# First projections dt by dt over half-loaded weights, another load order, and a last output tile in two halves, in a gated mix of local attention and a token MLP

## The chip, the core and the metric

The kernel runs on one core of one Trainium2 chip. The metric is the device time of one execution in microseconds (us). A profiled execution also has a span, from the first to the last instruction, which is about 1.7 us shorter than its time. Engines are written as in the profile: PE is the matmul engine, PEld its weight load, DVE the vector engine, ACT the scalar engine, POOL the general one, and SP the engine that issues the DMAs here (SPq is its queue). "Granted clock" is the share of PE's full clock that the throttle allowed, from the clock records of the trace. These begin when full clock is first granted (at 4.5 us in the kernel before); the half-speed matmuls before that are not in its mean, and a trace without such a record counts as 1.0.

Times of two kernels are compared only within the same rounds on the same chip. A ratio is the mean time of one kernel's fast runs over that of the other's of the same rounds, so it is not quite the ratio of the medians that are also quoted.

## The reference, cut to what matters

```python
# x: 2048 x 512 (bf16); 32 heads of 16; a window of 8 keys, two apart
g = sigmoid((x * gate_w).sum(-1))                # gate, one number per row
a = local_dilated_attention(x @ wqkv) @ wo       # softmax over 8 keys
h = layernorm(x)
u = gelu(h.T @ w1 + b1)                          # mixes tokens: 2048 -> 1792
b = (u @ w2 + b2).T                              # 1792 -> 2048
return g * a + (1 - g) * b
```

In the kernel, PE does in this order: transposes of the first 512 rows of x; the projections Q, K and V; bursts that reduce the products q*k (made by DVE) over each head; the first MLP matmul (14 tiles of 16 matmuls, called ph2); the second MLP matmul (16 output tiles of 14 matmuls, ph3), each tile followed by four attention matmuls with `wo` into the same PSUM bank. DVE does the products q*k, the layernorm, the softmax and the products attention*V. ACT evicts PSUM and does gelu and exp. W1 and W2 come in pieces of two tiles each through three buffers, so a later piece is loaded when the matmuls of an earlier one have ended.

## The kernel before

All operations are declared first; a list scheduler then fixes the order of instructions on each engine and DMA queue, from modelled durations, and waits are planned for that order. The order is thus decided when the kernel is built. Cuts are marked with `# ...`.

```python
# the scheduler: of all ready ops, the one that can start first; ties by longest path
k = (st, -bl[op.idx] + 3.0 * op.prio, op.idx)

# loads, in this order on the SP queue
ld_x("sp", 0, 4)
l_wq = ld_w("sp", 0, 0, 4)          # all of Wq
ld_w("sp", 1, 0, 4)                 # all of Wk
ld_x("sp", 4, 4)
ld_xt(1, deps=[l_wq])               # a transposing load of 512 rows
ld_x("sp", 8, 4); ld_xt(2); ld_x("sp", 12, 4); ld_xt(3)
# ...
# Q of the first 512 rows in matmuls of 256 columns, tile by tile
for tp_ in range(2):
    order0 = [(dt, tp_, dl) for dl in range(4) for dt in range(4)]
# ...
bank = main_bank()                  # projections rotate through three PSUM banks
# ...
# softmax: two exps over half the columns each, priced at 1.95 us, table load not priced
last_exp = A("act", ... func=AF.Exp, 1.95, name="sm_exp" + h, prio=0)
# gelu of each ph2 tile: another activation table than exp
A("act", ... func=AF.Gelu_apprx_tanh, 0.72, name="gel_%d" % ft, prio=0)
# attention weights, spread over partitions by DMA from SBUF to SBUF
ld_er(0, 4 * wh, 4, ["att_0", "att_1"], ...)             # chunk 0: waits for both exps
for c in range(1, 4):
    ld_er(c, 0, NW + 1, ["att_0", "att_1", "rs_0", "rs_1"], "er%d" % c, ...)
# W2 pieces; piece 4 and later reuse a buffer and wait for ph3
if i % 2 == 1 and j2 + 3 <= 7:
    ld_w2(j2 + 3)
```

## Time and profile before

| | before |
|---|---|
| time, median of 3 runs | 171.93 us |
| span of the profiled run (its time is 172.55 us) | 170.8 us |
| PE busy / granted clock | 165.0 us (97%) / 1.0 |
| DVE busy | 139.7 us (82%) |
| PE ends, DVE ends | 167.88 us, 161.47 us |

From the page of the kernel before: its header, the busy line, and the 40 equal slices of the span (busy tenths; PEclk is the granted clock in tenths).

```profile
span 170.8 us, 2127 instructions
PE 165.0 (97%) x876; PEld 78.6 (46%) x892; DVE 139.7 (82%) x118; ACT 66.2 (39%) x94; POOL 0.9 (1%) x8
PE   7999989999999999999999999999999999999993
PEclk9999999999999999999999999999999999999999
```

PE bounds the kernel: it is dense nearly everywhere. Two of the four waits of PE in the kernel before (engine and line, what it waited for, total us, times, longest); left out are 1.1 us at the very start and 0.2 us for which the profile names no cause:

```profile
PE ps L586 <- DMA arena<-in_A_x_dram: 0.5, 1, 0.5
PE ps L609 <- DMA arena<-in_A_wqkv_dram: 0.2, 1, 0.2
```

Little can be gained there. The timeline of ACT (start, length, line, operation, output and input, count):

```profile
75.37 1.28 ACT L727 ACT_TABLE_LOAD   x1
76.67 3.71 ACT L727 ACTIVATE arena<-arena 128x2048 bf16<-128x2048 bf16 x2
80.28 1.13 ACT L729 ACTIVATE arena<-arena 128x512 f32<-128x512 f32 x1
81.53 1.28 ACT L789 ACT_TABLE_LOAD   x1
```

Both exps run in a row behind one table load and end at 80.38 (76.67 + 3.71). The timeline of the SP queue: the length is the time that issuing took, not the transfer.

```profile
80.47 4.98 SPq L439 DMA_DIRECT2D arena<-arena  x8
85.49 5.65 SPq L439 DMA_DIRECT2D arena<-in_B_w_dram  x3
91.18 5.21 SPq L439 DMA_DIRECT2D arena<-arena  x4
96.43 0.58 SPq L439 DMA_DIRECT2D arena<-in_B_w_dram  x1
97.06 17.11 SPq L439 DMA_DIRECT2D arena<-arena  x12
114.22 10.02 SPq L439 DMA_DIRECT2D arena<-in_B_w_dram  x3
```

The first line is chunk 0 of the attention weights, released by the exps. Then come the last W1 piece with two W2 pieces, four small DMAs of softmax reciprocals, the third W2 piece, and chunks 1 to 3 of the attention weights. Only then, at 114.22, does the fourth W2 piece get its turn.

The view of this one DMA issue (`--source L439 --window 114.5:115.5`) has its time from issue to landing:

```profile
DMA to landing us min/median/max: 9.0/9.0/9.0
```

By the trace's completion records, which are finer, it landed at 123.19. It was 0.7 us early.

### The profile page before, as it was taken

The page shows a single profiled execution, that of the slowest core. Times are in us where ns is not written, and L with a number is a line of the kernel's source. Part 1 is how long each engine was busy: PE and PEld are TensorE (multiplying, and loading weights), DVE is VectorE, ACT ScalarE, POOL GpSimd, SP SyncE. Part 2 cuts the span into 40 slices and gives each one's busy share as a digit, 9 for nine tenths or more (in the row PEclk, how much of TensorE's full clock was granted, in tenths as well). Part 3 has the DMA queues.
Part 4 walks back from the last instruction along what each step waited for, and adds up shares of the span by engine and source line. Part 5 has one row for each costly group of instructions (what it writes and reads, how often), then busy time and mean ns, then how long its engine had stood idle before and what let it go on. Part 6 is the DMA issues. An engine that isn't in the chain of part 4 may idle for free.

```text
span 170.8 us, 2127 instructions
## 1 busy us (share of the span) xinstructions
PE 165.0 (97%) x876; PEld 78.6 (46%) x892; DVE 139.7 (82%) x118; ACT 66.2 (39%) x94; POOL 0.9 (1%) x8
## 2 busy tenths in 40 slices
PE   7999989999999999999999999999999999999993
PEld 2865544455444444444444444444444444444440
DVE  0745369999979999296999998899999999999800
ACT  3286656966458111569821122000011111122084
POOL 2000000000000000000000000000000000000000
PEclk9999999999999999999999999999999999999999
DMA  5999989960000053443989999998982818001023
GB/s 165 319 144 256 212 228 331 258 181 0 6 0 2 6 155 90 124 125 102 311 235 291 274 328 220 186 196 196 302 236 78 246 43 233 31 31 35 31 92 123
DMA packets 43101, 27.42 MB, mean 161 GB/s; under 512 B 7892, under 2 KB 42324, under 8 KB 42708
## 3 DMA queue, kind: packets, MB, share of 16 engines
q1 hardware_dynamic: 43092, 27.28, 62.5%
q8 instruction: 7, 0.11, 0.3%
q14 instruction: 2, 0.02, 0.0%
HBM read 18.88 MB, written 2.10 MB: 123 GB/s over the span
## 4 chain that ended last, share of the span: by engine, by line
PE 83%; DMA 7%; SPq 6%; ACT 2%; issue 1%
PE ps L776 28%; PE ps L840 28%; PE ps L586 14%; PE ps L849 8%; SPq L460 5%; PE ps L668 4%; DMA arena<-in_A_x_dram 4%; DMA arena<-in_A_wqkv_dram 3%; SPq L439 1%; ACT L564 1%; PE ps L638 1%; ACT arena L867 0%; ACT arena L594 0%; ACT arena L597 0%; ACT arena L564 0%
## 5 line engine op out<-in xcount | busy, mean ns | idle before, releaser
L816 DVE TENSOR_TENSOR arena<-arena 128x2048 bf16<-128x2048 bf16 (+2 forms) x32 | 71.5, 2287 | 1.8 <-DMA arena<-arena 1.5
L840 PE MATMUL ps<-arena 128*128 128x512 bf16 x220 | 49.8, 379 | 0.2
L776 PE MATMUL ps<-arena 128*128 128x512 bf16 x218 | 48.5, 379 | 0.3
L586 PE MATMUL ps<-arena 128*128 128x512 bf16 x171 | 38.3, 379 | 1.0 <-DMA arena<-in_A_x_dram 0.5
L661 DVE TENSOR_TENSOR arena<-arena 128x8192 bf16<-128x8192 bf16 x8 | 35.0, 4416 | 1.3 <-ACT arena L597 1.3
L840 PEld LDWEIGHTS ps<-arena 128*128 128x128 bf16 x224 | 21.9, 98 | 26.4
L776 PEld LDWEIGHTS ps<-arena 128*128 128x128 bf16 x224 | 21.7, 98 | 26.8 <-issue 0.8
L867 ACT ACTIVATE arena<-ps,arena 128x512 bf16<-128x512 f32 x16 | 12.4, 778 | 49.8 <-PE ps L849 49.3
L586 PEld LDWEIGHTS ps<-arena 128*128 128x128 bf16 x176 | 19.6, 114 | 19.1 <-ACT arena L594 0.9
L597 ACT ACTIVATE arena<-ps 128x512 bf16<-128x512 f32 x32 | 19.0, 598 | 7.1 <-PE ps L586 6.9
L789 ACT ACTIVATE arena<-ps,arena 128x512 bf16<-128x512 f32 x14 | 9.6, 687 | 30.8 <-PE ps L776 30.7
L551 DVE BATCH_NORM_STATS2 arena<-arena 128x6 f32<-128x512 bf16 x16 | 9.9, 681 | 6.9 <-DMA arena<-in_A_x_dram 6.9
L849 PE MATMUL ps<-arena 128*128 128x512 bf16 x63 | 15.4, 379 | 0.1
L849 PEld LDWEIGHTS ps<-arena 128*128 128x128 bf16 x64 | 6.3, 98 | 7.5
L713 DVE TENSOR_TENSOR arena<-arena 128x256 bf16<-128x256 bf16 (+4 forms) x16 | 7.9, 506 | 2.0 <-ACT arena L727 1.7
L594 ACT ACTIVATE arena<-ps 128x512 bf16<-128x512 f32 x12 | 7.2, 596 | 3.5 <-PE ps L586 3.5
L668 PE MATMUL ps<-arena 128*32 128x512 bf16 x128 | 7.5, 380 | 0.0
L698 ACT ACTIVATE arena<-ps 128x1024 bf16<-128x1024 f32 x4 | 4.0, 1021 | 5.0 <-PE ps L638 3.8
L570 DVE TENSOR_SCALAR arena<-arena 128x512 bf16<-128x512 bf16 x16 | 5.3, 407 | 0.0
L668 PEld LDWEIGHTS ps<-arena 128*32 128x32 bf16 x128 | 3.1, 96 | 4.1 <-DVE arena L713 0.4
L513 PE MATMUL ps<-arena 128*128 128x512 bf16 x9 | 4.0, 603 | 1.1 <-POOL arena L426 1.1
L609 PE MATMUL ps<-arena 128*128 128x256 bf16 x32 | 3.7, 273 | 0.2 <-DMA arena<-in_A_wqkv_dram 0.2
(50 smaller groups left out, 36.4 us busy)
## 6 DMA issues: line engine op xcount, KB each, us to landing
arena<-in_B_w_dram SPq DMA_DIRECT2D x7, 1024.0 KB, 6.4
arena<-in_B_w_dram SPq DMA_DIRECT2D x8, 896.0 KB, 6.8
arena<-arena SPq DMA_DIRECT2D x12, 288.0 KB, 5.9
arena<-in_A_x_dram SPq DMA_DIRECT2D x4, 512.0 KB, 4.9
out_dram<-arena SPq DMA_DIRECT2D x16, 128.0 KB, 1.7
arena<-in_A_wqkv_dram SPq DMA_DIRECT2D x3, 512.0 KB, 4.6
arena<-arena SPq DMA_DIRECT2D x8, 128.0 KB, 3.0
arena<-in_A_wo_dram SPq DMA_DIRECT2D x1, 512.0 KB, 9.2
```

Source lines behind the costliest of these rows:

```text
L460: return q_dma("sp", lambda e: e.dma_start_transpose(dst, src), 2 * SC * D * 2, "d_xt%d" % sb, ["xt_%d_%d" % (dt, sb) for dt in range(4)], ...
L551: A("dve", (lambda t_: (lambda e: e.bn_stats(out=ST6[:, t_, :], in_=X[:, t_, :])))(t), 0.7, reads=["x%d" % t], writes=["st6_%d" % t], name ...
L586: ins = e.matmul(ps[:, bank, :], lhsT=lhsT, rhs=XT[:, sb, dt, :], start=(dt == 0), stop=(dt == 3))
L597: return lambda e: e.activation(out=dst, in_=ps[:, bank, :], func=AF.Copy)
L661: return lambda e: e.tensor_tensor(out=PBL[buf], in0=in0, in1=in1, op=ALU.mult)
L668: ins = e.matmul(ps[32 * c:32 * c + 32, 4 + wl, :], lhsT=RP, rhs=PBL[buf][:, wl, c * 512:(c + 1) * 512], start=(dl == 0), stop=(dl == 3), ...
L776: ins = e.matmul(ps[:, bank, :], lhsT=W1W[:, slot, st, 128 * e_:128 * e_ + 128], rhs=X[:, st, :], start=(st == 0), stop=(st == NST - 1))
L789: A("act", (lambda ft_, bank_: (lambda e: e.activation(out=UT[:, ft_, :], in_=ps[:, bank_, :], func=AF.Gelu_apprx_tanh, bias=col(B1C, ft_) ...
L816: A("dve", lambda e: e.tensor_tensor(out=o_, in0=a_, in1=b_, op=op_), dur, reads=rd, writes=wr, name=nm)
L840: ins = e.matmul(ps[:, bank, :], lhsT=W2S[slot][:, ft, 128 * e_:128 * e_ + 128], rhs=UT[:, ft, :], start=(ft == 0), stop=False)
L849: ins = e.matmul(ps[:, bank, :], lhsT=OT[:, t, 128 * i:128 * i + 128], rhs=WO[:, t, :], start=False, stop=(t == 3))
L867: A("act", (lambda e, i=i, bank=bank: e.activation(out=OUTS[:, i, :], in_=ps[:, bank, :], func=AF.Identity, scale=col(OMG, i), bias=col(C2 ...
```

## The change

The intent: start the first projections when half of the Q weights have landed, keep PE fed until the transposed rows arrive, keep the evictions from stopping PE, and shorten the tail. The diff, cut to its core:

```diff
-        l_wq = ld_w("sp", 0, 0, 4)
-        ld_w("sp", 1, 0, 4)
+        ld_w("sp", 0, 0, 2)
+        l_wq = ld_w("sp", 0, 2, 2)
+        ld_w("sp", 1, 0, 2)
+        ld_w("sp", 1, 2, 2)
+        ld_xt(1, deps=[l_wq])
         ld_x("sp", 4, 4)
-        ld_xt(1, deps=[l_wq])
+        ld_xt(2)
         ld_x("sp", 8, 4)
-        ld_xt(2)
+        ld_xt(3)
         ld_x("sp", 12, 4)
-        ld_xt(3)
 # ... transposes and their evictions dt by dt instead of row tile by row tile; no second warm matmul
+        for tn in range(2):                       # Q and K of block 0, 512 columns each
+            for dt in range(4):
+                for dl in range(4):
 # ...
-        for dl in range(4):
-            for sb in range(2, 4):
-                seq_proj += [(0, dl, sb), (1, dl, sb)]
+        for (dl, sb) in ((0, 2), (1, 2), (0, 3), (1, 3), (2, 2), (2, 3), (3, 2), (3, 3)):
+            seq_proj += [(0, dl, sb), (1, dl, sb)]
-            bank = main_bank()
+            bank = (4, 5, 6, 7, 0, 1, 2)[k_ % 7] if k_ < 32 else main_bank()
 # ... second reduction burst split 3 + 1 instead of 2 + 2; ph2 tiles in four pieces instead of two
+            parts = [(bank, 0, D)] if i < NST - 1 else [(bank, 0, D // 2), (3, D // 2, D // 2)]
 # ... the last tile's second half is evicted by DVE, the first by ACT, each with its own DMA
```

The diff does not show what the scheduler makes of it. Built, the changed kernel has three differences in order that no line of the diff asks for:

1. On ACT, the sixth gelu now stands between the two softmax exps, with a table load on either side of it.
2. On the SP queue, the third W2 piece comes before the four small reciprocal DMAs, not after them.
3. On PE, the first reduction burst comes 16 matmuls later, because four V blocks moved ahead of it.

More of the change, by code (lines that the diff above doesn't have):

```diff
@@ L29 @@
 NWARM = 8
-NWARM2 = 1
 class _Op:
@@ L518, in bres, with f_tx @@
             return "acc%d" % b if b < 3 else "bank3" if b == 3 else "lg%d" % b
-        def f_tx(t):
+        def f_tx(dt):
             def fn(e):
                 ins = None
-                for dt in range(4):
-                    c0 = (dt % 2) * 256 + (t % 2) * 128
-                    ins = e.transpose(out=psb(4 * (t // 2) + 2 * (dt // 2) + 1)[:, c0:c0 + 128],
+                for t in range(4):
+                    ins = e.transpose(out=psb(2 * dt + 1)[:, 128 * t:128 * t + 128],
                                       in_=X[:, t, dt * 128:(dt + 1) * 128], identity=IDENT)
@@ L531, in bass_gated_mix__sliding_local_dilated__mixer_token_mlp__prompt_kernel @@
         front = A("pe", f_warm_on(NWARM, 0), 0.43 * NWARM, reads=["ones"], writes=["acc0"], name="warm", prio=-100)
-        for t in range(4):
-            tp = t // 2
-            front = A("pe", f_tx(t), 0.4, reads=["x%d" % t, "ident"], writes=[bres(4 * tp + 1), bres(4 * tp + 3)],
-                      after=[front], name="t_x%d" % t, prio=-100)
-            if t % 2 == 1:
-                for hb in range(2):
-                    src = sub(psb(4 * tp + 2 * hb + 1), 0, [(256, 2), (1, 256)])
-                    dst = sub(XT, 2 * hb * SC + tp * 256, [(SC, 2), (1, 256)])
-                    wr = ["xt_%d_0_%d" % (2 * hb + k, tp) for k in range(2)]
-                    if hb == 0:
-                        e_front = e_front + [A("dve", (lambda s_, d_: (lambda e: e.tensor_copy(out=d_, in_=s_)))(src, dst), 0.45,
-                          reads=[bres(4 * tp + 2 * hb + 1)], writes=wr, name="e_xt%d_%d" % (hb, tp), prio=-100)]
-                    else:
-                        A("act", (lambda s_, d_: (lambda e: e.activation(out=d_, in_=s_, func=AF.Copy)))(src, dst), 0.6,
-                          reads=[bres(4 * tp + 2 * hb + 1)], writes=wr, name="e_xt%d_%d" % (hb, tp), prio=-100)
-        XTALL = (["xt_%d_%d" % (dt, sb) for dt in range(4) for sb in range(1, 4)] +
-                 ["xt_%d_0_%d" % (dt, tp) for dt in range(4) for tp in range(2)])
+        for dt in range(4):
+            front = A("pe", f_tx(dt), 0.23, reads=["x%d" % t for t in range(4)] + ["ident"], writes=[bres(2 * dt + 1)],
+                      after=[front], name="t_x%d" % dt, prio=-100)
+            src = psb(2 * dt + 1)[:, 0:512]
+            dst = XT[:, 0, dt, :]
+            if dt % 2 == 0:
+                e_front.append(A("dve", (lambda s_, d_: (lambda e: e.tensor_copy(out=d_, in_=s_)))(src, dst), 0.45,
+                                 reads=[bres(2 * dt + 1)], writes=["xt_%d_0" % dt], name="e_xt%d" % dt, prio=-100))
+            else:
+                A("act", (lambda s_, d_: (lambda e: e.activation(out=d_, in_=s_, func=AF.Copy)))(src, dst), 0.6,
+                  reads=[bres(2 * dt + 1)], writes=["xt_%d_0" % dt], name="e_xt%d" % dt, prio=-100)
+        XTALL = ["xt_%d_%d" % (dt, sb) for dt in range(4) for sb in range(4)]
         for t in range(NST):
@@ L601, in xt_res, with f_proj1 @@
         def xt_res(sb):
-            if sb == 0:
-                return ["xt_%d_0_%d" % (dt, tp) for dt in range(4) for tp in range(2)]
             return ["xt_%d_%d" % (dt, sb) for dt in range(4)]
-        def f_proj1(dl, tp, bank, dt):
+        def f_proj1(tn, dl, bank, dt):
             def fn(e):
-                lhsT = sub(WQKV, dt * 3 * D + dl, [(4, 128)])
-                return e.matmul(ps[:, bank, 0:256], lhsT=lhsT, rhs=XT[:, 0, dt, 256 * tp:256 * tp + 256],
-                                start=(dt == 0), stop=(dt == 3))
+                lhsT = sub(WQKV, dt * 3 * D + tn * D + dl, [(4, 128)])
+                return e.matmul(ps[:, bank, :], lhsT=lhsT, rhs=XT[:, 0, dt, :], start=(dt == 0), stop=(dt == 3))
             return fn
@@ L616, in ev_proj @@
               writes=["%s5_%d_%d" % (tnames[tn], dl, sb)], name="ev_%s%d_%d" % (tnames[tn], dl, sb), prio=0)
-        last_main[0] = A("pe", f_warm_on(NWARM2, 0), 0.24 * NWARM2, reads=["ones"], writes=["acc0"], after=[front], name="warm2", prio=-100)
-        for tp_ in range(2):
-            order0 = [(dt, tp_, dl) for dl in range(4) for dt in range(4)]
-            for (dt, tp, dl) in order0:
-                b = 2 * dl + tp
-                last_main[0] = A("pe", f_proj1(dl, tp, b, dt), 0.12, reads=["xt_%d_0_%d" % (dt, tp), "wqkv0_%d" % dt],
-                                 writes=[bres(b)], after=[last_main[0]], name="pj0_%d_%d_%d" % (dl, dt, tp), prio=0)
-        for dl in range(4):
-            A("act", (lambda dl_: (lambda e: e.activation(out=Q5[:, dl_, 0:512], in_=sub(ps[:, 2 * dl_, :], 0, [(512, 2), (1, 256)]),
-                                                          func=AF.Copy, scale=0.25)))(dl), 0.62,
-              reads=[bres(2 * dl), bres(2 * dl + 1)], writes=["q5_%d_0" % dl], name="ev_q0_%d" % dl, prio=0)
+        last_main[0] = front
+        for tn in range(2):
+            for dt in range(4):
+                for dl in range(4):
+                    b = 2 * dl + tn
+                    last_main[0] = A("pe", f_proj1(tn, dl, b, dt), 0.216, reads=["xt_%d_0" % dt, "wqkv%d_%d" % (tn, dt)],
+                                     writes=[bres(b)], after=[last_main[0]], name="pj0_%d_%d_%d" % (tn, dl, dt), prio=0)
+            for dl in range(4):
+                ev_proj(tn, dl, 0, 2 * dl + tn)
         A("pe", f_tb, 0.3, reads=["b1r", "b2r", "gwr", "ident"], writes=["bank3"], name="t_b12", prio=-100, delay=2.0)
@@ L640, in f_gz @@
             return ins
-        seq_proj = [(1, dl, 0) for dl in range(4)]
+        seq_proj = []
         for dl in range(4):
             seq_proj += [(0, dl, 1), (1, dl, 1)]
-        for dl in range(4):
-            for sb in range(2, 4):
-                seq_proj += [(0, dl, sb), (1, dl, sb)]
+        for (dl, sb) in ((0, 2), (1, 2), (0, 3), (1, 3), (2, 2), (2, 3), (3, 2), (3, 3)):
+            seq_proj += [(0, dl, sb), (1, dl, sb)]
         seq_proj += [(2, dl, sb) for dl in range(4) for sb in range(4)]
-        for (tn, dl, sb) in seq_proj:
-            bank = main_bank()
+        for k_, (tn, dl, sb) in enumerate(seq_proj):
+            bank = (4, 5, 6, 7, 0, 1, 2)[k_ % 7] if k_ < 32 else main_bank()
             pj = A("pe", f_proj(tn, dl, sb, bank), 0.865,
                    reads=xt_res(sb) + ["wqkv%d_%d" % (tn, dt) for dt in range(4)],
-                   writes=["acc%d" % bank], after=[last_main[0]], name="pj_%s%d_%d" % (tnames[tn], dl, sb), prio=0)
+                   writes=[bres(bank)], after=[last_main[0]], name="pj_%s%d_%d" % (tnames[tn], dl, sb), prio=0)
             last_main[0] = pj
@@ L677, in bass_gated_mix__sliding_local_dilated__mixer_token_mlp__prompt_kernel @@
                   writes=["pb%d" % dl], name="qkm_%d_%d" % (wh, dl), prio=0)
-                if dl != 3 and (wh, dl) != (1, 1):
+                if dl != 3 and (wh, dl) != (1, 2):
                     continue
-                part = range(4) if wh == 0 else range(dl - 1, dl + 1)
+                part = range(4) if wh == 0 else range(3) if dl == 2 else range(3, 4)
                 def f_qk4(e, wh=wh, part=part):
@@ L684, in f_qk4 @@
                     return r + [f_gz(e)] if wh == 0 else r
-                A("pe", f_qk4, 4.6 if wh == 0 else 1.95, reads=["pb%d" % b for b in part] + ["rp"] + (XTALL + ["gwc"] if wh == 0 else []),
+                A("pe", f_qk4, 4.6 if wh == 0 else 0.95 * len(part), reads=["pb%d" % b for b in part] + ["rp"] + (XTALL + ["gwc"] if wh == 0 else []),
                   writes=["lg4", "lg5", "lg6", "lg7"] + (["bank3"] if wh == 0 else []), name="qkr_%d_%d" % (wh, dl), prio=-100, delay=BURST_DELAY)
@@ L768, in bass_gated_mix__sliding_local_dilated__mixer_token_mlp__prompt_kernel, with f_ph2 @@
         ld_er(0, NW, 1, ["rs_0", "rs_1"], "er0r")
-        def f_ph2(ft, bank, half):
+        def f_ph2(ft, bank, qu):
             slot = (ft // 2) % 3
@@ L774, in fn @@
                 ins = None
-                for st in range(8 * half, 8 * half + 8):
+                for st in range(4 * qu, 4 * qu + 4):
                     ins = e.matmul(ps[:, bank, :], lhsT=W1W[:, slot, st, 128 * e_:128 * e_ + 128], rhs=X[:, st, :],
@@ L783, in bass_gated_mix__sliding_local_dilated__mixer_token_mlp__prompt_kernel @@
             bank = main_bank()
-            p2 = A("pe", f_ph2(ft, bank, 0), 1.73, reads=["x%d" % t for t in range(NST)] + ["w1s%d" % (j % 3)],
-                   writes=["acc%d" % bank], after=[last_main[0]], name="ph2a_%d" % ft, prio=0)
-            p2 = A("pe", f_ph2(ft, bank, 1), 1.73, reads=["x%d" % t for t in range(NST)] + ["w1s%d" % (j % 3)],
-                   writes=["acc%d" % bank], after=[p2], name="ph2_%d" % ft, prio=0)
+            p2 = last_main[0]
+            for qu in range(4):
+                p2 = A("pe", f_ph2(ft, bank, qu), 0.865, reads=["x%d" % t for t in range(NST)] + ["w1s%d" % (j % 3)],
+                       writes=["acc%d" % bank], after=[p2], name="ph2_%d_%d" % (ft, qu), prio=0)
             last_main[0] = p2
@@ L831, in bass_gated_mix__sliding_local_dilated__mixer_token_mlp__prompt_kernel, with f_ph3 @@
                ["pp0"] + (["er0r_%d" % g for g in range(4)] if c == 0 else er_res(c, 0)), ["ot%d" % c], "avn_%d" % c)
-        def f_ph3(i, bank, half):
+        def f_ph3(i, bank, half, c0, nc_):
             slot = (i // 2) % 3
@@ L839, in fn @@
                 for ft in range(7 * half, 7 * half + 7):
-                    ins = e.matmul(ps[:, bank, :], lhsT=W2S[slot][:, ft, 128 * e_:128 * e_ + 128], rhs=UT[:, ft, :],
+                    ins = e.matmul(ps[:, bank, 0:nc_], lhsT=W2S[slot][:, ft, 128 * e_:128 * e_ + 128], rhs=UT[:, ft, c0:c0 + nc_],
                                    start=(ft == 0), stop=False)
@@ L843, in f_ph3, with f_wo @@
             return fn
-        def f_wo(i, bank):
+        def f_wo(i, bank, c0, nc_):
             def fn(e):
@@ L848, in fn @@
                 for t in range(4):
-                    ins = e.matmul(ps[:, bank, :], lhsT=OT[:, t, 128 * i:128 * i + 128], rhs=WO[:, t, :],
+                    ins = e.matmul(ps[:, bank, 0:nc_], lhsT=OT[:, t, 128 * i:128 * i + 128], rhs=WO[:, t, c0:c0 + nc_],
                                    start=False, stop=(t == 3))
@@ L859, in bass_gated_mix__sliding_local_dilated__mixer_token_mlp__prompt_kernel @@
             bank = YB[i % len(YB)]
-            br = bres(bank)
+            parts = [(bank, 0, D)] if i < NST - 1 else [(bank, 0, D // 2), (3, D // 2, D // 2)]
             for half in range(2):
-                last_main[0] = A("pe", f_ph3(i, bank, half), 1.515, reads=["ut%d" % ft for ft in range(7 * half, 7 * half + 7)] + ["w2s%d" % (j2 % 3)],
-                                 writes=[br], after=[last_main[0]], name="ph3%s_%d" % ("ab"[half], i), prio=0)
+                for (bk, c0, nc_) in parts:
+                    last_main[0] = A("pe", f_ph3(i, bk, half, c0, nc_), 1.515 * nc_ / D,
+                                     reads=["ut%d" % ft for ft in range(7 * half, 7 * half + 7)] + ["w2s%d" % (j2 % 3)],
+                                     writes=[bres(bk)], after=[last_main[0]], name="ph3%s_%d_%d" % ("ab"[half], i, c0), prio=0)
@@ L864, in bass_gated_mix__sliding_local_dilated__mixer_token_mlp__prompt_kernel @@
             if i % 2 == 1 and j2 + 3 <= 7:
                 ld_w2(j2 + 3)
-            A("pe", f_wo(i, bank), 0.865, reads=["ot%d" % (i // 4), "wo"], writes=[br], after=[last_main[0]], name="wo_%d" % i, prio=0)
-            A("act", (lambda e, i=i, bank=bank: e.activation(out=OUTS[:, i, :], in_=ps[:, bank, :], func=AF.Identity,
-                                                             scale=col(OMG, i), bias=col(C2, i))), 0.8,
-              reads=[br, "omg", "c2"], writes=["outs%d" % i] + (out_al if i == 0 else []), name="oev_%d" % i, prio=0)
@@ L870, in bass_gated_mix__sliding_local_dilated__mixer_token_mlp__prompt_kernel @@
-            sch.dma("sp", mk_dma(outv[:, i, :], OUTS[:, i, :]), 128 * D * 2, ds_out, issue=0.5, reads=["outs%d" % i], name="d_out%d" % i)
+            for (bk, c0, nc_) in parts:
+                A("pe", f_wo(i, bk, c0, nc_), 0.865 * nc_ / D, reads=["ot%d" % (i // 4), "wo"], writes=[bres(bk)], after=[last_main[0]],
+                  name="wo_%d_%d" % (i, c0), prio=0)
+                if c0 == 0:
+                    A("act", (lambda e, i=i, bk=bk, nc_=nc_: e.activation(out=OUTS[:, i, 0:nc_], in_=ps[:, bk, 0:nc_], func=AF.Identity,
+                                                                          scale=col(OMG, i), bias=col(C2, i))), 0.8 * nc_ / D,
+                      reads=[bres(bk), "omg", "c2"], writes=["outs%d_0" % i] + (out_al if i == 0 else []), name="oev_%d" % i, prio=0)
+                else:
+                    A("dve", (lambda e, i=i, bk=bk, c0=c0, nc_=nc_: e.tensor_scalar(out=OUTS[:, i, c0:c0 + nc_], in0=ps[:, bk, 0:nc_], scalar1=col(OMG, i),
+                                                                                    scalar2=col(C2, i), op0=ALU.mult, op1=ALU.add)), 0.45,
+                      reads=[bres(bk), "omg", "c2"], writes=["outs%d_%d" % (i, c0)], name="oev_%d_%d" % (i, c0), prio=0)
+                sch.dma("sp", mk_dma(outv[:, i, c0:c0 + nc_], OUTS[:, i, c0:c0 + nc_]), 128 * nc_ * 2, ds_out, issue=0.5,
+                        reads=["outs%d_%d" % (i, c0)], name="d_out%d_%d" % (i, c0))
```

## The prediction

> **What bounds the kernel now.** The page gives PE 165.0 of a 170.8 us span (97%) at full clock. The timeline shows PE dense from 6.03 us to 167.88 us except for four places: proj starts at 6.03 although the transposes end at 5.6 (waiting for the first Q weights, landed about 5.9); a spare warm matmul; about 0.5 us at 21.8, waiting for the last transposing x load (landed about 22.1); and about 1 us at 32.2–33.2, where a 1.28 us table load on ACT holds up evictions with only three banks in rotation (chain of waits). After PE: eviction 0.78, DMA about 1.7. DVE (82%) is second: it ends at 161.47, and the 13th output tile's attention matmuls, which need it, start at about 164.4. So DVE has only 3 us of slack.
>
> **Removed from PE.** Start 6.03 → about 5.65: 0.4. Q and K of block 0 as 32 matmuls of 216 ns instead of 32 of 114 plus 16 of 216, and no warm matmul: 0.4. The 22 us gap: 0.4. The 32 us gap, by rotating seven banks: 1.0. Added: perhaps 0.2 waiting for the first K evictions, and 0.2 for 36 half-width matmuls of 114 ns instead of 18 of 216. PE alone would end near 166.7, 1.2 us sooner. The tail saves about 0.25 us (ACT half about 0.56 instead of 0.78, an estimate from 0.60 us for 512 and 1.02 us for 1024 columns).
>
> **What I expect to eat it.** The instruction order on ACT changes in the softmax: before, one table load and both exps in a row (76.67–80.38); after, exp, table load, gelu, table load, exp. Two loads of 1.28 us (trace; the Trainium skill, "ScalarE: Activation LUTs", What ACT_TABLE_LOAD costs, also says about 1283 ns, and this trace agrees) and one gelu of 0.69 put the second exp's end at about 83.4, 3 us later. The eight attention-broadcast DMAs wait for both exps (80.47 → about 83.5), and all that is queued behind them (MLP weights, then chunk 1 of the attention weights, landed about 107.4, for which DVE waits 1.5 us) shifts by the same 3 us, the DMA engines being 80–90% busy there. DVE's own softmax sums also shift: first attention product 88.1 → about 90.8. Chunk 1 lands at about 110.4; DVE needs another 53.9 us (trace): ends at about 164.5 instead of 161.5. The 13th tile's attention matmuls want it at about 162.4 (4.3 us before PE's end). PE waits about 2 us, just before the end, and ends near 168.9.
>
> The later x loads delay the first DVE product by about 1.5 us, but PE's first reduction burst also comes 2 us later (four V blocks moved ahead of it), so this should not count.
>
> **Sum.** −1.2 (PE) +2.1 (new wait for DVE) −0.25 (tail) ≈ +0.6 us as worked out; I shade it, as the DVE/DMA shift may be less. Predicted 172.2 us, range 170.6 to 173.2. Faster by over 2%: 0.04; within 2%: 0.94; slower: 0.02.
>
> **What would show it.** Right: PE starts proj near 5.65; no PE gap at 22 and 32 us; the MLP matmuls start about 1.4 us sooner; second exp ends near 83.4; DVE's longest wait on SBUF-to-SBUF DMA near 108–110; DVE ends 163–165; the waits view shows PE waiting for DVE about 2 us before the last attention matmuls. Wrong: DVE ends below 162.4 and PE has no gap at the end; then time would be about 170.2. Also wrong: a PE wait near 9–11 us, K weights held up behind the transposing load.
>
> **What would make it wrong.** Attention weights landing sooner than a rigid 3 us shift; transposing loads landing late.

## More of the kernel before

From the chain of work that ended last, in the kernel before:

```profile
105.71 9.06 PE ps L840 x42
114.78 0.05 issue
114.83 10.52 PE ps L840 x48
```

These are ph3 matmuls, without a gap. The fourth W2 piece is first used by the 85th of them, at about 105.71 + 84 x 0.216 = 123.9.

## The result, and the profile after

The changed kernel took 178.66 us (median of 4 runs, 177.46 to 179.42) against 172.3 us. The ratio is 1.036 (95% interval 1.029 to 1.043): slower by 3.6%, outside the predicted range of 170.6 to 173.2. From the page of the changed kernel (its profiled run was the fastest of the four):

```profile
span 175.7 us, 2151 instructions
PE 167.0 (95%) x893; PEld 79.2 (45%) x893; DVE 140.3 (80%) x119; ACT 68.2 (39%) x96; POOL 0.9 (0%) x8
PE   7999999999999999999999999998099999999994
PEclk9999999999999999999999999999969999999999
```

There is a hole in PE in the 29th slice, and a lower clock right after it. The waits of PE in the changed kernel, without the 1.1 us at the very start:

```profile
PE ps L829 <- DMA arena<-in_B_w_dram: 5.0, 1, 5.0
```

The two small waits of before are gone; there is one large new one. The chain of work that ended last, in the changed kernel:

```profile
104.16 14.20 PE ps L829 x66
118.37 8.92 DMA arena<-in_B_w_dram
127.28 0.05 issue
127.33 3.17 PE ps L829 x7
130.50 0.95 PE ps L838 x4
```

The second MLP matmul starts at 104.16, 1.55 us sooner than before, so the front gained what it should. At 122.3 PE stops for a W2 piece whose issue began at 118.37 and which landed at 127.28. The next 7 matmuls take 3.17 us; 7 of them should take 1.51 (7 x 0.216). The timeline of ACT in the changed kernel:

```profile
74.74 1.28 ACT L716 ACT_TABLE_LOAD   x1
76.03 1.91 ACT L716 ACTIVATE arena<-arena 128x2048 bf16<-128x2048 bf16 x1
77.96 1.28 ACT L778 ACT_TABLE_LOAD   x1
79.26 0.69 ACT L778 ACTIVATE arena<-ps,arena 128x512 bf16<-128x512 f32 x1
79.96 1.28 ACT L716 ACT_TABLE_LOAD   x1
81.26 1.91 ACT L716 ACTIVATE arena<-arena 128x2048 bf16<-128x2048 bf16 x1
```

The second exp ends at 83.17, 2.8 us later than before. The timeline of the SP queue in the changed kernel:

```profile
83.26 5.00 SPq L438 DMA_DIRECT2D arena<-arena  x8
88.30 8.93 SPq L438 DMA_DIRECT2D arena<-in_B_w_dram  x4
97.27 21.05 SPq L438 DMA_DIRECT2D arena<-arena  x16
118.37 8.31 SPq L438 DMA_DIRECT2D arena<-in_B_w_dram  x3
```

Everything starts 2.8 us later, and the fourth W2 piece 4.15 us later (118.37 against 114.22). The buffer it goes into had been free since about 110.2 (104.16 + 28 matmuls of 0.216 us); for 8 us it only stood behind 16 other DMAs. The clock, from the windows view of the changed kernel: a stretch in us, its length, busy time and count for PE, PEld, DVE, ACT and POOL, then granted clock, DMA share and GB/s.

```profile
124.00:126.00 2.00, 0.00 (x0) 0.00 (x0) 2.00 (x3) 0.00 (x0) 0.00 (x0) 1.00 0.92 277
126.00:128.00 2.00, 0.67 (x2) 0.28 (x3) 1.97 (x2) 0.00 (x0) 0.00 (x0) 0.79 1.18 314
128.00:130.00 2.00, 2.00 (x6) 0.74 (x5) 1.93 (x3) 0.00 (x0) 0.00 (x0) 0.50 1.19 290
130.00:132.00 2.00, 2.00 (x10) 0.82 (x9) 2.00 (x1) 0.51 (x1) 0.00 (x0) 0.86 0.96 237
```

By the clock records it was half for 3.41 us, which cost 1.66 us on these 7 matmuls (3.17 - 1.51). Of this, 0.17 us is the restart after a wait: where the clock did not fall, the same 7 took 1.68 us (experiments 1 and 6). PE ended 5.28 us later than before (173.15 against 167.87): front -1.55, wait +5.04, lower clock +1.66, and +0.13 that is left for the half-width matmuls of the last tile and the end of the slow stretch. From PE's end to the end of the span took 2.58 us instead of 2.92, so the tail is -0.34. Together that is +4.94, and the spans differ by 4.95. The other three runs were 0.9 to 2.0 us longer than this one. Their mean granted clock was 0.98 instead of 0.99, which fits a half-clock stretch of twice the length: the profiled run of experiment 5, with a mean clock of 0.981, has one of 6.83 us.

### The profile page after: what moved, and what is told of

Its sections match the earlier page's. It is cut to its first block, busy times and chain, and to the rows that moved or that the text cites. A ratio compares the mean times of both kernels' runs of the same rounds, so it can differ in the third digit from the quotient of the medians.

```text
span 175.7 us, 2151 instructions
## 1 busy us (share of the span) xinstructions
PE 167.0 (95%) x893; PEld 79.2 (45%) x893; DVE 140.3 (80%) x119; ACT 68.2 (39%) x96; POOL 0.9 (0%) x8
## 4 chain that ended last, share of the span: by engine, by line
PE 93%; DMA 5%; ACT 0%; issue 0%; POOL 0%; POOLq 0%
PE ps L765 28%; PE ps L829 26%; PE ps L581 20%; PE ps L838 8%; DMA arena<-in_B_w_dram 5%; PE ps L657 4%; PE ps L602 4%; PE ps L514 2%; PE ps L525 1%; PE ps L628 0%; ACT arena L861 0%; POOL arena L425 0%; PE ps L506 0%; PE ps L508 0%; PE ps L507 0%
## 5 line engine op out<-in xcount | busy, mean ns | idle before, releaser
L829 PE MATMUL ps<-arena 128*128 128x512 bf16 (+1 forms) x238 | 51.8, 374 | 5.0 <-DMA arena<-in_B_w_dram 5.0
L765 PE MATMUL ps<-arena 128*128 128x512 bf16 x224 | 48.9, 379 | 0.0
L581 PE MATMUL ps<-arena 128*128 128x512 bf16 x160 | 35.1, 379 | 0.0
L861 ACT ACTIVATE arena<-ps,arena 128x512 bf16<-128x512 f32 (+1 forms) x16 | 12.2, 764 | 56.6 <-PE ps L838 56.2
L592 ACT ACTIVATE arena<-ps 128x512 bf16<-128x512 f32 x32 | 18.4, 597 | 7.4 <-PE ps L581 6.0
L778 ACT ACTIVATE arena<-ps,arena 128x512 bf16<-128x512 f32 x14 | 9.6, 687 | 22.7 <-PE ps L765 22.5
L838 PE MATMUL ps<-arena 128*128 128x512 bf16 (+1 forms) x68 | 15.7, 368 | 0.0
L589 ACT ACTIVATE arena<-ps 128x512 bf16<-128x512 f32 x16 | 9.2, 599 | 5.2 <-PE ps L581 2.9
L602 PE MATMUL ps<-arena 128*128 128x512 bf16 x32 | 7.1, 380 | 0.0
L865 DVE TENSOR_SCALAR arena<-ps,arena 128x256 bf16<-128x256 f32 x1 | 0.5, 543 | 7.5 <-PE ps L838 7.5
```

Of the source, the lines that this page charges most:

```text
L581: ins = e.matmul(ps[:, bank, :], lhsT=lhsT, rhs=XT[:, sb, dt, :], start=(dt == 0), stop=(dt == 3))
L592: return lambda e: e.activation(out=dst, in_=ps[:, bank, :], func=AF.Copy)
L602: return e.matmul(ps[:, bank, :], lhsT=lhsT, rhs=XT[:, 0, dt, :], start=(dt == 0), stop=(dt == 3))
L765: ins = e.matmul(ps[:, bank, :], lhsT=W1W[:, slot, st, 128 * e_:128 * e_ + 128], rhs=X[:, st, :], start=(st == 0), stop=(st == NST - 1))
L778: A("act", (lambda ft_, bank_: (lambda e: e.activation(out=UT[:, ft_, :], in_=ps[:, bank_, :], func=AF.Gelu_apprx_tanh, bias=col(B1C, ft_) ...
L829: ins = e.matmul(ps[:, bank, 0:nc_], lhsT=W2S[slot][:, ft, 128 * e_:128 * e_ + 128], rhs=UT[:, ft, c0:c0 + nc_], start=(ft == 0), stop=False)
```

## The experiments

All outputs are right. Most edits act on the finished schedule: `move(engine, op, ref)` takes one operation out of one engine's list and puts it behind another one; the modelled times are then worked out again and the waits planned as always. So nothing but this order changes. Theory A: the late second exp delays a whole queue of DMAs, and the first to run out of slack is the fourth W2 piece, not DVE. The rivals are named in the texts. In the table, the time is the median of all runs, while the ratio leaves out runs marked slow (one each in "before, exps apart" and "changed, reciprocals first").

| kernel | time, us | before | ratio (95%) |
|---|---|---|---|
| changed kernel | 178.66 | 172.30 | 1.036 (1.029 to 1.043) |
| changed, exps together | 173.63 | 172.43 | 1.009 (1.004 to 1.014) |
| changed, fourth W2 piece ahead | 176.10 | 172.43 | 1.020 (1.017 to 1.024) |
| changed, both moves | 170.83 | 172.43 | 0.992 (0.990 to 0.994) |
| before, exps apart | 177.85 | 172.43 | 1.029 (1.022 to 1.037) |
| changed, reciprocals first | 176.48 | 172.15 | 1.021 (1.013 to 1.028) |
| changed, gap filled | 176.23 | 172.15 | 1.025 (1.022 to 1.029) |
| changed, exps together, reciprocals first | 171.64 | 172.15 | 0.997 (0.995 to 0.999) |
| both moves, chunk 1 ahead | 170.68 | 172.09 | 0.992 (0.990 to 0.994) |
| both moves, whole tail | 172.34 | 172.09 | 1.001 (0.999 to 1.003) |
| both moves again | 171.04 | 172.09 | 0.994 (0.992 to 0.997) |
| both moves, whole tail again | 171.51 | 172.04 | 0.997 (0.995 to 0.999) |
| both moves, third time | 171.14 | 172.04 | 0.994 (0.991 to 0.997) |

### 1. The exps together again

```diff
+ move("act", "gel_5", "g_ezc")      # the sixth gelu behind both exps and the gate's exps
```

> The changed kernel, with one move in ACT's order: the sixth gelu goes behind both exps and the two gate exps, as in the kernel before; two table loads fewer, nothing else moved. Theory A (the second exp, 3 us late behind a gelu and two table loads, delays the attention-weight DMAs and with them the fourth W2 load on the same queue): second exp ends near 80.1 us instead of 83.2, the fourth W2 load is issued near 115.3 instead of 118.4 and lands near 124.2; PE's wait for it falls from 5.0 us to about 1.9; DVE ends near 162.2; time about 173 us. Rival B (the wait comes from the changed order of the loads on the queue, whatever ACT does): the fourth W2 load is still issued near 118, the wait stays near 5 us, time 178.

Measured: 173.63 us. The exps ended at 80.28, the fourth W2 piece was issued at 115.72 and landed at 124.53. The waits of PE in this kernel:

```profile
PE ps L859 <- DMA arena<-in_B_w_dram: 1.9, 1, 1.9
```

The wait fell from 5.0 to 1.9 us, as theory A had it to a tenth. One gelu in another place, on an engine that is busy 39% of the time, takes most of the loss back (ratio 1.009 instead of 1.036). Rival B (queue order alone, whatever ACT does) falls; what the order adds is tried in experiments 5 and 7. The clock stayed at 1.0 in three of four runs; the fourth had 0.99 and took 175.11 us.

### 2. The fourth W2 piece ahead of the last chunk

```diff
+ move("sp", "d_w2_3", "d_er3_0", before=True)
```

> The changed kernel, with one move in the DMA queue: the fourth W2 load is issued before the four DMAs of the last attention-weight chunk instead of after them; ACT's order stays (exps apart). Theory A: the load is issued near 112.5 us and lands near 120.5, before PE wants it at 122.3, so the 5.0 us wait and the lowered clock vanish; what is left is the wait that the prediction named: DVE ends near 165.3, PE wants it near 162.3, so PE waits about 3 us before the 13th tile's attention matmuls; time about 173.3 us. Rival D (the wait is for DMA bandwidth, not for the issue behind other issues): the load lands no sooner than about 125 and PE still waits over 2 us at 122; time over 175.

Measured: 176.1 us. The fourth piece landed at 122.09 and PE had no wait at 122. But the waits of PE, and the chain at the end, show the wait that the prediction had named, in its place:

```profile
PE ps L868 <- DVE arena L835: 3.5, 1, 3.5
```

```profile
165.21 1.24 DVE arena L835
166.49 4.45 PE ps L868 x12
170.94 0.76 PE ps L859 x7
```

DVE ended at 166.45 and PE waited 3.5 us for it. Then the clock fell here too: 12 matmuls took 4.45 us instead of 2.6, 1.86 us more. The expected 173.3 us had left out the clock, and in this profiled run full clock also came late at the start, at 6.5 us. So the predicted mechanism is real, but it stood behind a larger one and had been priced too low. Rival D falls as it is worded: the same load, issued 5.0 us sooner, landed 5.2 us sooner. It took 8.7 us from issue to landing, against 8.9 in the changed kernel. What this does not rule out is that bandwidth sets the pace of the whole queue: the DMA share from 97 to 118.4 us is 1.05 in the changed kernel (windows view).

### 3. Both moves

```diff
+ move("act", "gel_5", "g_ezc")
+ move("sp", "d_w2_3", "d_er3_0", before=True)
```

> Both moves together on the changed kernel. Theory A: no PE wait over 0.5 us either at 122 or before the 13th tile (DVE ends near 162.2, PE wants it near 162.4); what is left is the gain of the change on PE; span about 169.3, time about 170.3 us, faster than both kernels. If other parts of the change cost time too: over 172.

Measured: 170.83 us, ratio 0.992, with no PE wait after the start and clock 1.0 in all runs. With both orders mended, the change is a gain of 0.8% (0.6% in experiments 10 and 12). No other part of it costs time that this run could show.

### 4. The exps apart, in the kernel before

```diff
+ move("act", "gel_5", "sm_exp_0")   # on the kernel before: the sixth gelu behind the first exp
```

> The kernel before, with one move in ACT's order: the sixth gelu goes between the two softmax exps (two more table loads), as the change has it; nothing else of the change. Theory A: second exp ends 3 us later (about 83.4 us), the fourth W2 load is issued near 117.2 instead of 114.2 and lands near 126.2, while PE wants it at 124.0: PE waits about 2.3 us, and if the clock drops as in the changed kernel, up to 1.7 us more; time 174.5 to 176.3 us. Rival E (the loss needs the new front or the new load order): time stays within 0.5 us of 172.3.

The built orders were compared: PE, DVE and the DMA queue are those of the kernel before, only ACT's differs. (The two traces agree with this: PE's weight loads, DVE and the DMA queue come in the same order.) Measured: 177.85 us. The waits of PE and the chain:

```profile
PE ps L870 <- DMA arena<-in_B_w_dram: 2.4, 1, 2.4
```

```profile
117.18 8.85 DMA arena<-in_B_w_dram
126.03 0.05 issue
126.08 3.17 PE ps L870 x7
```

The wait was 2.4 us (2.3 expected) and the next 7 matmuls took 3.17 us: the clock fell after a gap of only 2.4 us. So two table loads and a gelu in the wrong place are enough to make the old kernel as slow as the changed one, without any new front, load order or tail. Rival E falls. The time exceeds the expected 176.3 us because two of the four runs had a lower mean clock (0.981, which fits twice the half-clock time; 178.9 and 179.4 us). The two others took 176.4 and 176.8 us.

### 5. The reciprocals first

```diff
+ move("sp", "d_w2_2", "d_er0r_3")   # third W2 piece behind the reciprocals, as before
```

> The changed kernel, with one move in the DMA queue: the third W2 load goes behind the four small reciprocal DMAs, as in the kernel before (the change had put it ahead of them); ACT's order stays (exps apart). If the wait of 5.0 us is 3.1 from the late exp, 1.3 from this swap and 1.3 from the earlier PE, less 0.8 of slack: the fourth W2 load is issued near 117.1 us, lands near 126.0, PE waits about 3.7 us and the clock still drops; time about 177 us against 178.7. If the swap is innocent: the wait stays 5 us.

Measured: 176.48 us. The fourth W2 piece was issued at 117.88 and landed at 126.68. The wait of PE for it:

```profile
PE ps L859 <- DMA arena<-in_B_w_dram: 4.0, 1, 4.0
```

(The profile fell into a slow run. Its clock fell at 125.1, while PE was already waiting, so the wait itself is not longer for it.) By PE's wait the swap in the queue is worth 1.0 us here (5.0 to 4.0), a little under the 1.3 that was expected. The time of issue alone, 117.88 against 118.37, would understate it: this whole run was about 0.4 us later than the changed kernel's by then (second exp's end 83.60 against 83.17, PE's stop 122.72 against 122.29). The swap also holds up chunk 1: without it DVE's last attention product ended at 163.6 instead of 165.3. The four runs also sort by their clock: 174.09 us at a mean clock of 1.0, 176.47 and 176.48 at 0.99, 177.82 at 0.981; how long the gap was in each of them is not known.

### 6. The gap filled with useless matmuls

```diff
+ if i == 6:      # 23 matmuls of ones into PSUM bank 3, just ahead of the ones that wait
+     last_main[0] = A("pe", f_warm_on(23, 3), ..., reads=["ones"], writes=["bank3"], after=[last_main[0]])
```

> The changed kernel, with 23 useless matmuls of 512 columns (ones into PSUM bank 3, unused then) put into the PE gap, right before the first matmul that waits for the fourth W2 load; 23 x 0.216 = 5.0 us, as long as the wait. Data and orders elsewhere stay. If a part of the loss is the lowered clock after the idle time: the next 7 matmuls take 1.5 us instead of 3.2, the mean granted clock is 1.0 in every run, time about 176.2 us with a spread under 1 us (the changed kernel: 177.5 to 179.4). If the clock falls for another reason (power, DMA load), clock and time stay as they were.

Measured: 176.23 us, three runs within 0.05 us and one at 177.3, clock 1.0 in all. The chain:

```profile
118.75 8.83 DMA arena<-in_B_w_dram
127.63 1.68 PE ps L860 x7
```

The load lands as late as ever, but the 7 matmuls behind it take 1.68 us instead of 3.17. So here the clock falls because PE is idle, and not because of power or DMA load. By the ratios (1.025 against 1.036) this second cost is about 1% of the time, 1.8 us on average.

### 7. The exps together and the reciprocals first

```diff
+ move("act", "gel_5", "g_ezc")
+ move("sp", "d_w2_2", "d_er0r_3")
```

> The changed kernel with the exps together (first experiment) and the third W2 load behind the reciprocal DMAs, but the fourth W2 load left behind the last attention chunk. By the sum of parts the fourth load lands near 123.2, PE wants it near 122.6: a wait of about 0.6 us, no clock loss, DVE no longer the limit; time about 171.5 us. If the swap is innocent, it repeats the 173.6 us and the 1.9 us wait of the first experiment.

Measured: 171.64 us. The fourth W2 piece landed at 123.22, 1.3 us sooner than in the first experiment, although the exps ended 0.3 us later in this run. The wait of PE for it:

```profile
PE ps L859 <- DMA arena<-in_B_w_dram: 0.3, 1, 0.3
```

By PE's wait the swap is worth 1.6 us here (1.9 to 0.3); with the late exps it was worth 1.0. Why the two differ was not tried.

### 8. Chunk 1 ahead of the third W2 piece

```diff
+ move("act", "gel_5", "g_ezc")
+ # ... the declared rule "chunk 1 is issued after the third W2 load" is dropped first
+ move("sp", "d_w2_2", "d_er1_3")
+ move("sp", "d_w2_3", "d_er3_0", before=True)
```

> The kernel with both moves, plus a third: the third W2 load goes behind the four DMAs of the second attention chunk, so that this chunk lands near 104 us instead of 108 and DVE does not wait about 3 us for it; DVE should end near 159.4 instead of 162.2, about 3 us ahead of PE's need. If PE alone bounds the kernel with both moves, time stays within 0.3 us of it (about 170.7); if DVE's end still held PE back there, 0.3 to 0.5 us sooner.

Measured: 170.68 us (170.54 to 171.28) against 171.04 us with both moves. DVE no longer waited for attention weights and ended at 159.3, with 3 us to spare. The difference of 0.3 us is within the spread of the runs, so this is called a gain in slack, not in time. Its ratio to the kernel before is 0.992, where the changed kernel has 1.036.

### 9 and 10. The last tile whole, and both moves again

```diff
- parts = [(bank, 0, D)] if i < NST - 1 else [(bank, 0, D // 2), (3, D // 2, D // 2)]
+ parts = [(bank, 0, D)]
```

> The kernel with both moves, but the last output tile whole again, evicted by ACT alone. PE ends about 0.2 us sooner (18 matmuls of 216 ns instead of 36 of about 114), and from PE's end to the end of the span takes 2.9 us instead of 2.55: time about 0.15 to 0.2 us longer than with the halves, 170.9 to 171.1. If the halves do nothing: no difference.

> The kernel with both moves again, as the yardstick for the two others of this call: 170.7 us, 0.8% faster than the kernel before, no PE wait over 0.2 us after the start, clock 1.0 in every run.

Measured: 172.34 us whole, 171.04 us in halves. The 1.3 us were far more than the expected 0.2. The spans of the profiled runs differ by 1.5 us. Of this, 0.8 us sat at the very start: full clock began at 6.8 us in one and at 5.1 us in the other, and the projections of the later rows began at 13.53 instead of 12.75. The tail cannot do that. The other 0.7 us lay after PE's end: from there to the end of the span took 3.32 us whole and 2.58 in halves.

### 11 and 12. The same pair again

> The kernel with both moves and the whole last tile once more, because in its first trial 0.8 us of the 1.5 us by which its profiled run was longer sat at the start, where full clock came at 6.8 us instead of 5.1. If the whole tail itself costs what its own lines say (eviction 0.78 instead of 0.56 us, PE 0.2 us less): 0.2 to 0.5 us slower than the kernel with halves of the same call. If the tail costs the whole 1.3 us: again 172.3 against 171.0.

> The kernel with both moves and the last tile in halves, unchanged, as the yardstick for the whole tail in this call: 170.8 to 171.1 us.

Measured: 171.51 us whole, 171.14 us in halves. This time full clock began at 3.8 us in the profiled run of the whole tail, and from PE's end to the end of the span took 3.32 us whole and 2.59 in halves. But the profiled run in halves (171.68 us) had another loss:

```profile
PE ps L868 <- DVE arena L835: 0.8, 1, 0.8
```

This is the wait that the prediction had named, with both moves in place. The other two profiled runs of this kernel do not have it, so its DVE is at the edge, and the slack that experiment 8 gains is of use. By the times the halves are worth about 0.4 us here; the intervals of the two ratios overlap, so neither the size nor, by this pair alone, the sign is settled. By the traces of both pairs they save 0.7 us after PE's end, and the start of both pairs, with DVE in the second, covers the rest of the differences. Of the 0.7 us, 0.4 lies after the last store has landed (0.78 us to the end of the span whole, 0.40 in halves); why is not known, and the kernel before, whose last tile is whole too, has 0.39 there.

## Why the prediction was wrong

Most of the steps held, and to a few tenths:

- PE's front: projections predicted to start near 5.65, measured 5.60 by the chain; no PE gap at 22 and 32 us; MLP matmuls predicted about 1.4 us sooner, measured 1.55 (51.92 against 53.47 for the first of ph2).
- The softmax: second exp predicted to end near 83.4, measured 83.17; attention DMAs at about 83.5, measured 83.26; first attention product at about 90.8, measured 90.36.
- DVE: predicted to end at about 164.5, measured 165.3, because chunk 1 landed at 111.25 and not at 110.4; without the swap of the reciprocals it ended at 163.6 (experiment 5).
- The tail: 0.25 us predicted, 0.34 in the profile (2.92 to 2.58 after PE's end).

The step that failed is the one headed "What I expect to eat it". The text says that "all that is queued behind them" shifts by 3 us, and then follows only one of the delayed transfers, chunk 1, to its user DVE, and concludes that PE waits "about 2 us, just before the end". The fourth W2 piece stands behind the chunks on the same queue. It had a slack of 0.7 us before (landed 123.2, wanted 123.9), was delayed by 4.1 us (127.3), and PE now wanted it 1.55 us sooner: 4.1 + 1.55 - 0.7 is about 5.0, the measured wait. It comes 40 us before the predicted one and hides it. Experiment 1 shows that 3.1 of the 5.0 us are the exps; experiment 4 shows that the exps alone are enough.

A second term was missing from the sum: the granted clock after a wait. With the restart it cost 1.66 us in the profiled run and, as an estimate, about twice that in runs with a mean clock of 0.98. The prediction counted even its own wait without it; experiment 2, which lays that wait bare, measured 3.5 us of waiting plus 1.86 us of restart and lower clock where the prediction had 2.1 us in all. So with the W2 piece out of the way the prediction would still have been too low, by two mis-sized terms.

The prediction's doubt also pointed the wrong way. It shaded its sum down because "the DVE/DMA shift may be less"; what ought to have been asked is what else uses the shifted queue.

Why did the scheduler put the gelu between the exps? It takes what can start first, and it knows no table loads. When the changed kernel is built again and the modelled times are printed, the first exp ends at 77.09, the input of the second is ready at 77.16 and the gelu is ready before, so the gelu goes first and holds the second exp up by 0.65 us in the model. In the trace the second exp starts 3.3 us after the first one ends (77.94 to 81.26). Variants that were built but never run on the chip tell how thin the decision is: with the burst split 2 + 2 or the ph2 tiles in two pieces, the sixth gelu goes ahead of both exps; with the old order of the Q and K blocks, it goes behind both. No single line of the change can be blamed.

## What to carry to other kernels

When a change delays one entry of an in-order DMA queue, list every transfer behind it with its slack (when it is wanted less when it lands), not only the one you have in mind; a transfer that is never waited for can still be 0.7 us from the critical path. Add the cost of PE's clock to a PE wait of the size seen here: with the restart it was 1.7 us or more in each profiled run with a wait of 2.4 to 5 us that was not filled, and only the 0.2 us of the restart in the one with a wait of 1.9 us; where the limit lies was not measured. After every change to a kernel whose order comes from a scheduler, compare the built orders and count the table loads: two more, with a gelu between the exps, on an engine that is 39% busy, made the old kernel 2.9% slower.

## What the Trainium skill lacked or had wrong

- "TensorE: Matmul & The Clock Gate", What's actually happening, says that PE falls to half clock after at least one idle window of about 3.4 us. The half-clock stretches here were 3.41 us long, and 6.83 in experiment 5, which fits whole windows. But a wait of 2.4 us was enough (experiment 4: half clock from 125.75, of the 3.41 us before that PE was idle for about 2.1), while a wait of 1.9 us did not do it in the profiled run of experiment 1. So a window need not be wholly idle; the rule of the same page, "HAM oscillation", of no gaps over about 3.4 us is too generous.
- The same page says that the start of full clock varies with the free-running window, by 500 ns either way. The runs agree that it varies, but by more: where the trace records it, it began between 3.8 and 6.8 us after the start of the span, with PE's first matmul always at 1.05 to 1.06, and the projections of the later rows moved by up to 1.1 us (12.28 to 13.37). What the page does not spell out is that this is enough to spoil a comparison of kernels that differ by under 1% (experiments 9 to 12).
- "ScalarE: Activation LUTs", What ACT_TABLE_LOAD costs, gives 1283 ns for the load and about 1380 ns more for a drain, 2.66 us for each switch. The load took 1.28 us here, but no drain shows: exp ended at 77.94, the load ran from 77.96, and the gelu started at 79.26. A switch cost 1.3 us, half of what the page says.
- "DMA: Bandwidth & Descriptors", Issuing engines are not separate DMA queues, says that the time to initiate a DMA "is usually small relative to the DMA itself". Here 16 issues in a row took 21.05 us and held up a load whose buffer was free for 8 us; the 12 equal DMAs of 288 KB among them took 0.59 to 2.34 us each to issue, against 4.2 to 6.5 us from issue to landing. The page lacks the point that issues can grow this long on a busy queue, so that a load's place in the queue is a delay. What makes them grow was not tried here.
